# Attention, MoE and routed MoE on one core: the first MoE's cosine as one shifted sine, and the high halves of odd score tiles on ScalarE

## The chip, the cores and the metric

The kernel runs on one core of one Trainium2 chip, as one program. The metric is the time of an execution in microseconds (us), measured on the device. The engines are named as the profile names them: PE is TensorE's matmul, PEld its weight load, DVE is VectorE, ACT is ScalarE, POOL is GpSimd, SP is SyncE, which here only issues DMAs.

## The reference, cut to what matters

```python
# u, v: 8 x 3072 x 256; z: 8 x 3072 x 64
scores = np.matmul(z, z.transpose(0, 2, 1)) / S
out = np.matmul(np.maximum(scores, 0.0) ** 2, v)
x = (u * out).reshape(B * S, D)                  # 24576 tokens x 256
h = x @ w_in                                     # first MoE: 256 -> 2048
x = (h * np.cos(h)) @ w_out                      # 2048 -> 256
# second MoE: every token goes to one of 8 experts (256 -> 1024 -> 256),
# chosen by cosine similarity, with relu, and is scaled by its gate
out[mask] = gate_w[mask, None] * (np.maximum(x[mask] @ w1[e], 0.0) @ w2[e])
```

## The kernel before

**Arithmetic.** All large products are done in fp16 with each factor split in a high half and a low half (hi = round(x), lo = x - hi), and three matmuls for each product: hi*hi, hi*lo, lo*hi. So each product's left factor costs two more passes on the other engines: one that makes the high half, one that subtracts it.

**Tiling.** Tokens are taken in 48 chunks of 512, n = 0 to 47, six to each of the eight batches; c = n mod 6 is the chunk's place in its batch. A chunk's attention needs 24 score tiles of 128 x 512, j = 0 to 23. Scores are symmetric, so chunk c computes only the tiles j = 4c to 23 and reads the others back, transposed, from a copy that an earlier chunk wrote to DRAM. Of the computed tiles the first four lie on the diagonal and are narrower (512, 384, 256, 128 columns).

- A computed tile goes through `att_S` (PE, PSUM tile `sc`), `att_relu` (ACT, L547), `att_a32` (the square, ACT, L554), `att_ahi` (the high half, L569 or L571), `att_alo` (the low half, DVE, L577), and `att_V` (PE, `acc`, L641 to L643).
- A chunk's first MoE runs two chunks later, in 16 slices f of 128 hidden units: `ffn_H` (six matmuls, L709 to L711, into PSUM tile `h`, which has two buffers), `ffn_k` (ACT, L718: h in turns, rounded to an integer), `ffn_f` (DVE, L724: the fraction of a turn), `ffn_sin` (ACT, L731), `ffn_sq` (ACT, L735), `ffn_g` (DVE, L739: (2 sin^2 - 1) * h, which frees `h`), `ffn_ghi` (ACT, L746), `ffn_glo` (DVE, L752), `ffn_O` (twelve matmuls, L767 to L775).
- Then comes the chunk's readout: `ro_evac`, `ro_scale`, `ro_hi`, `ro_lo` build the row that is stored, `ro_T` (SP) transposes it by DMA, `ro_tail` (DVE, L839 and L840) writes the row's tail and must wait until these transposes (`xrT`) have read it, and `ro_logits` and `ro_rank` route the tokens.
- Once per batch, at the end of the batch before, `v_scale` finds the scale of v: a sum on DVE, an all-reduce over partitions on POOL (behind the index scatters of `ro_rank`), and nine small DVE instructions that wait for it (the first is L118).

The second MoE starts after the last chunk, at about 4000 us of the span.

**Order.** The program is written as a list of events with a nominal time each (`tl.at(t, function, n, f)`), sorted by that time, and given to a tile framework. After the first stretch SP's order is the list's; the other engines' instructions are placed by the framework's scheduler, which starts from the list. On the chip each engine runs its instructions strictly in the order in which they stand, so an instruction that waits holds up all that stand behind it.

Of the kernel before, what the change touches and what calls it, by code (L numbers as in the profile page):

```python
# [8 lines left out]
FP32 = mybir.dt.float32  # L9
FP16 = mybir.dt.float16  # L10
I32 = mybir.dt.int32
ACTF = mybir.ActivationFunctionType
ALU = mybir.AluOpType
AX = mybir.AxisListType
PI = 3.141592653589793
# [26 lines left out]
def kernel(  # L42
# [15 lines left out]
    nc = tc.nc  # L58
# [19 lines left out]
    const = ctx.enter_context(tc.tile_pool(name="const", bufs=1))  # L78
# [70 lines left out]
    en_r = const.tile([128, KD, 2 * E], FP16, name="en_r")  # L149
    ienx = const.tile([128, 1], FP32, name="ienx")  # L150
    zrow = const.tile([1, RW // 2], FP32, name="zrow")

    tl = Timeline()

# [40 lines left out]
    def setup_consts():  # L195
        nc.gpsimd.memset(ones16, 1.0)
        ii = small.tile([128, 128], FP32, name="ii", tag="ii")
        nc.gpsimd.iota(
            ii, pattern=[[1, 128]], base=0, channel_multiplier=-1, allow_small_or_imprecise_dtypes=True
        )  # L200

        nc.vector.tensor_scalar(out=lt16, in0=ii, scalar1=0.0, scalar2=None, op0=ALU.is_gt)
        nc.gpsimd.iota(tok_i, pattern=[[CH, NC], [128, TT]], base=0, channel_multiplier=1)
        e_f = small.tile([128, TT, E], FP32, name="e_f", tag="e_f")
        nc.gpsimd.iota(
            e_f, pattern=[[0, TT], [1, E]], base=0, channel_multiplier=0, allow_small_or_imprecise_dtypes=True
        )
        nc.vector.tensor_scalar(
            out=wfirst, in0=e_f, scalar1=-1.0, scalar2=float(E), op0=ALU.mult, op1=ALU.add
        )  # L210
        nc.vector.tensor_scalar(
            out=ecap, in0=e_f[:, 0, :], scalar1=float(CAP), scalar2=None, op0=ALU.mult
        )
        nc.vector.tensor_copy(out=base, in_=ecap)
        nc.vector.memset(zrow, 0.0)
        nc.sync.dma_start(out=xs_d[NT:NT + 1, :], in_=zrow)
        rows = E * CAP + CH
        fill = st_p.tile([128, 512], I32, name="fill", tag="st")
        nc.gpsimd.memset(fill, NT)
        blk = 128 * 512  # L220
        r0 = 0
        while r0 < rows:
            n = min(blk, rows - r0)
            c = n // 128
            nc.sync.dma_start(
                out=idl_d[r0:r0 + n, :].rearrange("(p c) o -> p (c o)", p=128), in_=fill[:, 0:c]
            )
            r0 += n
# [61 lines left out]
    wsc = {}  # L290
# [241 lines left out]
    def att_cols(n, j):  # L532

        return slice((j % 4) * 128 if j // 4 == n % NCB else 0, CH)
# [22 lines left out]
    def att_ahi(n, j):  # L557

        hl = at_p.tile([128, 2 * CH], FP16, name="ahl", tag="ahl", bufs=8)
        a = a_t[n, j]  # L560
        if j // 4 == n % NCB:
            hl = hl.rearrange("p (w c) -> p w c", w=2)
            hi, lo = (hl[:, w, att_cols(n, j)] for w in range(2))
        else:
            a = a.rearrange("p (t c) -> p t c", c=128)
            hl = hl.rearrange("p (t w c) -> p t w c", w=2, c=128)
            hi, lo = (hl[:, :, w] for w in range(2))
        if n < 2 and j % 2:
            nc.scalar.activation(out=hi, in_=a, func=ACTF.Copy)  # L569
        else:  # L570
            nc.vector.tensor_copy(out=hi, in_=a)  # L571
        a_t[n, j] = (a, hi, lo, hl)
# [44 lines left out]
    def att_order(c):  # L617

        load, off = list(range(4 * c)), list(range(4 * c + 4, NJ))

        at = 4 if c else 0
        comp, off = off[:at], off[at:]
        for j in range(4 * c, 4 * c + 4):
            comp += [j, *off[:2]]
            off = off[2:]
        comp += off
        pos = [((i + 0.5) / len(x), j) for x in (load, comp) for i, j in enumerate(x)]
        return [j for _, j in sorted(pos)]
# [19 lines left out]
    u_t, x_t, xsc = {}, {}, {}  # L648
# [49 lines left out]
    h_t, f_t, g_t, o_t = {}, {}, {}, {}  # L698
# [15 lines left out]
        h_t[n, f] = ps  # L714

    def ffn_k(n, f):
        kt = ff_p.tile([128, CH], I32, name="kt", tag="kt", bufs=5)
        nc.scalar.activation(out=kt, in_=h_t[n, f], func=ACTF.Copy, scale=xsc[n][0])  # L718
        f_t[n, f] = kt

    def ffn_f(n, f):
# [4 lines left out]
        )  # L726
        f_t[n, f] = t

    def ffn_sin(n, f):
        t = f_t[n, f]  # L730
        nc.scalar.activation(out=t, in_=t, func=ACTF.Sin, scale=PI)  # L731

    def ffn_sq(n, f):
        t = f_t[n, f]
        nc.scalar.activation(out=t, in_=t, func=ACTF.Square, scale=2.0 ** 0.5)  # L735

    def ffn_g(n, f):
        g = f_t.pop((n, f))
        nc.vector.scalar_tensor_tensor(  # L739
            out=g, in0=g, scalar=1.0, in1=h_t.pop((n, f)), op0=ALU.subtract, op1=ALU.mult  # L740
        )
        g_t[n, f] = [g]

    def ffn_ghi(n, f):
# [38 lines left out]
    def ro_evac(n):  # L783
        x2 = ro_p.tile([128, TT, D], FP32, name="x2", tag="x2")
        o = o_t.pop(n)
        k2 = small.tile([128, 1], FP32, name="k2", tag="k2")
        nc.vector.tensor_scalar(
            out=k2, in0=xsc[n][1], scalar1=wsc[1][1], scalar2=-1.0, op0=ALU.mult, op1=ALU.mult
        )
        for t in range(0, TT, 2):  # L790
            nc.scalar.activation(  # L791
                out=x2[:, t:t + 2], in_=o[TT + t // 2], func=ACTF.Copy, scale=k2
            )
        x2_t[n] = x2
# [151 lines left out]
    def tB(n):  # L946
        return starts[n]

    tl.at(30000, setup_consts)
    for b in range(B):  # L950
        n0 = b * NCB
        if b == 0:
            tl.at2(3700, 3700, z_nat, z_stat, 0)
            for c in range(NCB):
                t = 8600 + 1400 * c if c < 2 else 4000 + 7000 * c
# [10 lines left out]
        else:  # L966
# [7 lines left out]
            for c in range(NCB):  # L974

                t = last + (min((c - NCB + 2) * ZC, 0.1) + (c == NCB - 1) * 0.9) * P
# [23 lines left out]
    for n in range(NC):  # L1000
        t0 = tB(n)
        st = (tB(n + 1) - t0) / NJ
        tl.at(t0 + 0.3 * NJ * st, u_load, n)
        order = att_order(n % NCB)
        for i, j in enumerate(order):
            t = t0 + i * st
            if j // 4 < n % NCB:
                tl.at(t + LV - LM, att_load, n, j)
            else:

                ts = max(t0, t - DV * st) if j // 4 == n % NCB and j % 4 else t
                tl.at(ts, att_S, n, j)
                tl.at(ts + 300, att_relu, n, j)
                tl.at(ts + 1500, att_a32, n, j)
                tl.at(ts + 2000, att_ahi, n, j)
                tl.at(ts + 2400, att_alo, n, j)
                tl.at(max(ts + 6000, t + LV - 5500), att_mirror, n, j)


            if i in (0, NJ - 2):  # L1020
                continue
            js = order[i - 1:i + 1] if i in (1, NJ - 1) else [j]
            tl.at(t + LV + (0, 1000, 700, 0)[min(i, 3)], att_V, n, js, i == 1, i == NJ - 1)
        e = tB(n + 1) - st + LV + 1400
        tl.at(e, x_mul, n)
        tl.at(e + 5000, x_scale, n)
        for k in range(KD):
            tl.at(e + 5500 + 1500 * k, x_hi, n, k)
            tl.at(e + 6500 + 1500 * k, x_lo, n, k)

        tail = n + 2 - NC
        fb = tB(n + 2) + 14000 if tail < 0 else tB(NC) + 12000 + tail * PF
        FP = (tB(n + 3) - tB(n + 2) if tail < 0 else PF) / NF
        LO = (3.2 if tail >= 0 else 3.00) * FP
        for f in range(NF):
            t = fb + f * FP
            tl.at(t, ffn_H, n, f)
            tl.at(t + 1400, ffn_k, n, f)
            tl.at(t + 1800, ffn_f, n, f)
            tl.at(t + 3200, ffn_sin, n, f)  # L1040
            tl.at(t + 3900, ffn_sq, n, f)
            tl.at(t + 4700, ffn_g, n, f)
            tl.at(t + 6600, ffn_ghi, n, f)
            tl.at(t + 8300, ffn_glo, n, f)
            tl.at(t + LO, ffn_O, n, f)
        r = fb + (NF - 1) * FP + LO + 1500
        tl.at(r, ro_evac, n)
        tl.at(r + 2300, ro_scale, n)
        for t in range(TT):
            tl.at(r + 3000 + 2000 * t, ro_hi, n, t)  # L1050
            tl.at(r + 4200 + 2000 * t, ro_lo, n, t)

        late = RT if tail < 0 else 4000.0
        for t in range(TT):
            tl.at(r + 4300 + 2000 * t + late, ro_T, n, t)
        tl.at(r + 11500 + late, ro_tail, n)
        tl.at(r + 17000 + late, ro_logits, n)
        tl.at(r + 27000 + late, ro_rank, n)
        T_RANK[n] = r + 27000 + late
        T_END = r  # L1060
# [303 lines left out]
    for s, (tb, i, n) in enumerate(slots):  # L1364
# [13 lines left out]
        for u in range(nu):  # L1378
            t = t0 + u * fq
# [55 lines left out]
```

## Time and profile before

| | us |
|---|---|
| median of three runs | 5095.66 (5089.55 to 5098.19) |
| the profiled execution | 5086.35 |
| its span, first to last instruction | 5084.6 |
| PE busy | 4885.2 (96% of the span) |
| DVE busy | 3641.9 (72%) |
| ACT busy | 3302.5 (65%) |
| POOL busy | 1509.3 (30%) |

The profile is one execution; its own time is 1.75 us more than its span and 9.3 us under the median of the runs. Busy time says how long an engine worked, waits say which engine it stood still for. An engine's waits matter only if the engine itself is one that the end waits for.

### The profile page before, as it was taken

The numbers are of one execution on the slowest core, as the hardware profiler recorded it, in microseconds if no ns is written. First come the engines' busy times: TensorE is split into PE (matmuls) and PEld (weight loads), VectorE is DVE, ScalarE is ACT, GpSimd is POOL, SyncE is SP. The second block draws the span as 40 slices with busy tenths as digits, with TensorE's granted clock in tenths as the row PEclk, the third lists the DMA queues.
The fourth block names the chain that finished last, engine by engine and source line by source line (L and its number), as shares of the span: only waits on it lengthen the run. The fifth ranks groups of instructions, "written<-read, shape, count | busy, mean of one in ns | idle before, by whom it ended". The sixth has DMA issues, their size and how long they took to land.

```text
span 5084.6 us, 87365 instructions
## 1 busy us (share of the span) xinstructions
PE 4885.2 (96%) x31032; PEld 2935.5 (58%) x31032; DVE 3641.9 (72%) x9258; ACT 3302.5 (65%) x6269; POOL 1509.3 (30%) x2105
## 2 busy tenths in 40 slices
PE   6999999999999999999999999999999799999999
PEld 2555555555555555555555555555556467777776
DVE  6967776777678768776877787777767655656565
ACT  6777777777778778777877787777767422222222
POOL 3232222232233223223322322332121333333332
PEclk9999999999999999999999999999999899999999
DMA  7676468456755675647555844774472667777874
GB/s 225 172 144 119 110 138 135 115 122 132 132 122 130 121 137 121 131 100 151 130 114 111 161 125 95 142 137 111 99 124 54 174 180 212 212 213 219 226 224 129
DMA packets 963689, 731.26 MB, mean 144 GB/s; under 512 B 855696, under 2 KB 858769, under 8 KB 954418
## 3 DMA queue, kind: packets, MB, share of 16 engines
q1 hardware_dynamic: 835490, 351.44, 36.0%
q0 software_dynamic: 127760, 374.24, 26.8%
q8 instruction: 243, 3.98, 0.4%
q14 instruction: 196, 1.61, 0.1%
HBM read 315.17 MB, written 215.19 MB: 104 GB/s over the span
## 4 chain that ended last, share of the span: by engine, by line
PE 63%; ACT 12%; DVE 12%; issue 6%; DMA 5%; POOL 1%; SPq 1%; POOLq 0%; another core or an unknown queue 0%; DVEq 0%; ACTq 0%
PE acc L642 6%; PE acc L643 6%; PE acc L641 6%; PE o L771 4%; PE o L775 4%; PE h L709 4%; PE o L767 4%; PE h L710 4%; PE h L711 4%; PE h L1297 3%; PE o L1334 3%; PE o L1327 3%; PE o L1331 3%; PE h L1289 3%; PE h L1293 3%
## 5 line engine op out<-in xcount | busy, mean ns | idle before, releaser
L767 PE MATMUL o<-wo,gh 128*128 128x256 f16 x3072 | 841.0, 274 | 5.3 <-ACT x L791 4.1
L775 PE MATMUL o<-wo,gl 128*128 128x256 f16 x3072 | 840.6, 274 | 1.7 <-DVE gl L752 1.2
L771 PE MATMUL o<-wo,gh 128*128 128x256 f16 x3072 | 841.4, 274 | 0.0
L746 ACT ACTIVATE gh<-kt 128x512 f16<-128x512 f32 x768 | 482.4, 628 | 458.8 <-DVE kt L739 445.0
L739 DVE SCALAR_TENSOR_TENSOR kt<-kt,h 128x512 f32<-128x512 f32 x768 | 525.9, 685 | 344.1 <-ACT kt L735 332.7
L752 DVE TENSOR_TENSOR gl<-kt,gh 128x512 f16<-128x512 f32 x768 | 528.5, 688 | 223.9 <-ACT gh L746 206.9
L731 ACT ACTIVATE kt<-kt 128x512 f32<-128x512 f32 x768 | 480.4, 626 | 313.0 <-DVE kt L724 303.1
L580 POOL DMA_DIRECT2D at_d<-ahl x480 | 268.5, 559 | 1286.7 <-DVE ahl L577 1044.7
L709 PE MATMUL h<-xh,wi 128*128 128x512 f16 x1536 | 587.6, 383 | 37.8 <-DVE kt L739 36.7
L724 DVE SCALAR_TENSOR_TENSOR kt<-h,c,kt 128x512 f32<-128x512 f32 x768 | 572.9, 746 | 63.3 <-ACT kt L718 59.1
L1306 ACT ACTIVATE hh<-h 128x512 f16<-128x512 f32 x398 | 234.9, 594 | 567.7 <-PE h L1297 470.7
L710 PE MATMUL h<-xl,wi 128*128 128x512 f16 x1536 | 587.5, 382 | 0.0
L711 PE MATMUL h<-xh,wi 128*128 128x512 f16 x1536 | 586.8, 382 | 0.0
L718 ACT ACTIVATE kt<-h,c 128x512 int32<-128x512 f32 x768 | 517.5, 674 | 105.6 <-PE h L711 86.3
L642 PE MATMUL acc<-ahl,vh 128*128 128x512 f16 x1344 | 512.3, 381 | 38.9 <-DVE ahl L577 38.8
L641 PE MATMUL acc<-ahl,vh 128*128 128x512 f16 x1344 | 511.2, 381 | 14.2 <-ACT vh L363 5.7
L1308 DVE SCALAR_TENSOR_TENSOR hl<-h,hh 128x512 f16<-128x512 f32 x398 | 271.7, 687 | 336.8 <-ACT hh L1306 307.4
L643 PE MATMUL acc<-ahl,vl 128*128 128x512 f16 x1344 | 511.7, 381 | 0.0
L735 ACT ACTIVATE kt<-kt 128x512 f32<-128x512 f32 x768 | 481.1, 626 | 14.4
L1334 PE MATMUL o<-w,hl 128*128 128x256 f16 x1592 | 435.4, 274 | 18.0 <-DVE hl L1308 14.2
L1331 PE MATMUL o<-w,hh 128*128 128x256 f16 x1592 | 435.2, 273 | 4.4 <-issue 4.4
L1327 PE MATMUL o<-w,hh 128*128 128x256 f16 x1592 | 435.1, 273 | 3.9 <-issue 3.8
(326 smaller groups left out, 10510.5 us busy)
## 6 DMA issues: line engine op xcount, KB each, us to landing
w<-we_d SPq DMA_DIRECT2D x69, 2048.0 KB
at_d<-ahl POOLq DMA_DIRECT2D x480, 256.0 KB
vst<-in_v POOLq DMA_DIRECT2D x168, 256.0 KB
est<-in_w POOLq DMA_DIRECT2D x128, 256.0 KB
xs_d<-row POOLq DMA_DIRECT2D x48, 544.0 KB
ut<-in_uT POOLq DMA_DIRECT2D x42, 512.0 KB
zst<-in_zT POOLq DMA_DIRECT2D x84, 128.0 KB
ad_d<-ahl POOLq DMA_DIRECT2D x96, 96.0 KB
```

The source lines that it names most:

```text
L641: nc.tensor.matmul(out=acc[k], lhsT=h, rhs=ah, start=beg, stop=False)
L642: nc.tensor.matmul(out=acc[k], lhsT=h, rhs=al, start=False, stop=False)
L643: nc.tensor.matmul(out=acc[k], lhsT=lo, rhs=ah, start=False, stop=end)
L709: nc.tensor.matmul(out=ps, lhsT=wi_hi[:, k, fs], rhs=xh[:, k], start=(k == 0), stop=False)
L710: nc.tensor.matmul(out=ps, lhsT=wi_hi[:, k, fs], rhs=xl[:, k], start=False, stop=False)
L711: nc.tensor.matmul(out=ps, lhsT=wi_lo[:, k, fs], rhs=xh[:, k], start=False, stop=(k == KD - 1))
L767: nc.tensor.matmul(out=o[t], lhsT=gh[:, ts], rhs=wo_hi[:, f], start=(f == 0 and t % 2 == 0), stop=False, skip_group_check=True,)
L771: nc.tensor.matmul(out=o[t], lhsT=gh[:, ts], rhs=wo_lo[:, f], start=False, stop=False, skip_group_check=True,)
L775: pe_last[0] = nc.tensor.matmul(out=o[t], lhsT=gl[:, ts], rhs=wo_hi[:, f], start=False, stop=(f == NF - 1), skip_group_check=True,).ins
L1327: nc.tensor.matmul(out=o[t], lhsT=hh[:, ts], rhs=wh, start=(f == 0 and t % 2 == 0), stop=False, skip_group_check=True,)
L1331: nc.tensor.matmul(out=o[t], lhsT=hh[:, ts], rhs=wl, start=False, stop=False, skip_group_check=True)
L1334: nc.tensor.matmul(out=o[t], lhsT=hl[:, ts], rhs=wh, start=False, stop=(f == NF2 - 1), skip_group_check=True,)
```

## The change

The cosine was made as 1 - 2 sin^2: h is turned into a fraction of a turn in -0.5 to 0.5, ACT takes sin(pi f), squares it with a factor sqrt(2), and DVE computes (that - 1) * h, whose sign the readout's scale `k2` turns back. Now `ffn_k` adds a quarter turn before it rounds, so that the fraction lies in -0.75 to 0.25, ACT takes sin(2 pi f + pi/2) once, and DVE multiplies by h. The quarter and pi/2 are bias operands that stand in SBUF, one number for each partition. `ffn_sq` is gone, and the nominal times of the steps after the sine are 700 ns earlier. Besides, `att_ahi` of odd tiles, which was on ACT only in the first two chunks, is on ACT in all chunks.

```diff
+    quarter = const.tile([128, 1], FP32, name="quarter")
+    half_pi = const.tile([128, 1], FP32, name="half_pi")
...
+        nc.vector.memset(quarter, 0.25)
+        nc.vector.memset(half_pi, PI / 2.0)
...
-        if n < 2 and j % 2:
+        if j % 2:
             nc.scalar.activation(out=hi, in_=a, func=ACTF.Copy)
         else:
             nc.vector.tensor_copy(out=hi, in_=a)
...
-        nc.scalar.activation(out=kt, in_=h_t[n, f], func=ACTF.Copy, scale=xsc[n][0])
+        nc.scalar.activation(
+            out=kt, in_=h_t[n, f], func=ACTF.Identity, scale=xsc[n][0], bias=quarter
+        )
...
-        nc.scalar.activation(out=t, in_=t, func=ACTF.Sin, scale=PI)
-        nc.scalar.activation(out=t, in_=t, func=ACTF.Square, scale=2.0 ** 0.5)
+        nc.scalar.activation(out=t, in_=t, func=ACTF.Sin, scale=2.0 * PI, bias=half_pi)
...
-        nc.vector.scalar_tensor_tensor(
-            out=g, in0=g, scalar=1.0, in1=h_t.pop((n, f)), op0=ALU.subtract, op1=ALU.mult
-        )
+        nc.vector.tensor_tensor(out=g, in0=g, in1=h_t.pop((n, f)), op=ALU.mult)
...
-            out=k2, in0=xsc[n][1], scalar1=wsc[1][1], scalar2=-1.0, op0=ALU.mult, op1=ALU.mult
+            out=k2, in0=xsc[n][1], scalar1=wsc[1][1], scalar2=None, op0=ALU.mult
...
-            tl.at(t + 4700, ffn_g, n, f)
+            tl.at(t + 4000, ffn_g, n, f)
```

The order of PE's matmuls stays nearly the same, and SP's stays the same. DVE's and ACT's orders move at many places. Three of them follow; line numbers in the changed program are two to eight higher.

DVE, at the readout of chunk 7 (c = 1; the same at the other seven chunks with c = 1). Before, with `ffn_g` (L739), a score tile's high half (L571), the row's tail (L839, L840), the same tile's low half (L577), `ffn_glo` (L752) and `ffn_f` (L724):

```order
L739 SCALAR_TENSOR_TENSOR kt<-kt,h 128x512
L571 CAST ahl<-r 128x4x128
L839 COPY row<-amv 128x4x4
L840 COPY row<-ssq 128x4x4
L577 TENSOR_TENSOR ahl<-r,ahl 128x4x128
L752 TENSOR_TENSOR gl<-kt,gh 128x512
L724 SCALAR_TENSOR_TENSOR kt<-h,c_8057,kt 128x512
```

The same place in the changed program (`ffn_g` is L743, `ffn_glo` L754, the low half L581, `ffn_f` L731, the tail L841 and L842):

```order
L743 TENSOR_TENSOR kt<-kt,h 128x512
L754 TENSOR_TENSOR gl<-kt,gh 128x512
L581 TENSOR_TENSOR ahl<-r,ahl 128x4x128
L731 SCALAR_TENSOR_TENSOR kt<-h,c_7950,kt 128x512
L407 TENSOR_REDUCE ewm<-ewst 128x2
L841 COPY row<-amv 128x4x4
L842 COPY row<-ssq 128x4x4
L743 TENSOR_TENSOR kt<-kt,h 128x512
```

The tile is odd, so its high half is no longer here, and its low half, `ffn_glo` and `ffn_f` stand ahead of the tail, not behind it.

DVE, at the readout of chunk 20 (c = 2; the same at chunks 2, 8, 14, 32 and 38, not at 26). Before:

```order
L724 SCALAR_TENSOR_TENSOR kt<-h,c_20570,kt 128x512
L752 TENSOR_TENSOR gl<-kt,gh 128x512
L364 SCALAR_TENSOR_TENSOR vl_21822<-vst,vss,vh_21821 128x512
L839 COPY row<-amv 128x4x4
L840 COPY row<-ssq 128x4x4
L739 SCALAR_TENSOR_TENSOR kt<-kt,h 128x512
```

The changed program (L368 is the low half of a piece of v, as L364 was):

```order
L754 TENSOR_TENSOR gl<-kt,gh 128x512
L841 COPY row<-amv 128x4x4
L368 SCALAR_TENSOR_TENSOR vl_21488<-vst,vss,vh_21487 128x512
L731 SCALAR_TENSOR_TENSOR kt<-h,c_20255,kt 128x512
L842 COPY row<-ssq 128x4x4
L743 TENSOR_TENSOR kt<-kt,h 128x512
```

Here it is the other way round: `ffn_f` of the slice (L731) and the split of v, which stood ahead of the tail, now stand behind its first instruction; the slice's `ffn_g` is the last row in both.

ACT, at the start of batch 4 (chunk 24). Before, with `ffn_k` (L718), two splits of z (L363), `ffn_sin`, `ffn_sq`, `ffn_ghi` (L746), and the first tiles' relu (L547), square (L554):

```order
L363 ACTIVATE r_5_22308<-zst,zps 64x512
L731 ACTIVATE kt<-kt 128x512
L735 ACTIVATE kt<-kt 128x512
L746 ACTIVATE gh<-kt 128x512
L718 ACTIVATE kt<-h,c_20570 128x512
L547 ACTIVATE r<-sc 128x512
L547 ACTIVATE r<-sc 128x384
L554 ACTIVATE r<-r 128x512
L554 ACTIVATE r<-r 128x384
L731 ACTIVATE kt<-kt 128x512
L547 ACTIVATE r<-sc 128x512
```

The changed program (`ffn_cos` is L739, `ffn_k` L723, `ffn_ghi` L748, relu L551, square L558, the high half L573):

```order
L367 ACTIVATE r_5_21963<-zst,zps 64x512
L739 ACTIVATE kt<-kt,half_pi 128x512
L748 ACTIVATE gh<-kt 128x512
L723 ACTIVATE kt<-h,quarter,c_20255 128x512
L551 ACTIVATE r<-sc 128x512
L551 ACTIVATE r<-sc 128x384
L558 ACTIVATE r<-r 128x512
L558 ACTIVATE r<-r 128x384
L739 ACTIVATE kt<-kt,half_pi 128x512
L573 ACTIVATE ahl<-r 128x384
L551 ACTIVATE r<-sc 128x512
```

One instruction fewer stands in front of the first relu; in front of the third the copy of the odd tile has come in.

## Rows read from the trace of the kernel before

**Rows 1.** The page: busy us, share of span, instructions of each engine.

```profile
PE 4885.2 (96%) x31032; PEld 2935.5 (58%) x31032; DVE 3641.9 (72%) x9258; ACT 3302.5 (65%) x6269; POOL 1509.3 (30%) x2105
```

**Rows 2.** Windows: stretch, its length, busy us (count) by engine, clock, DMA, GB/s.

```profile
0.00:200.00 200.00, 145.81 (x660) 66.26 (x661) 144.45 (x313) 139.42 (x262) 66.16 (x113) 0.97 0.78 218
200.00:3900.00 3700.00, 3609.60 (x21732) 2068.81 (x21730) 2788.66 (x6168) 2805.45 (x5305) 1036.70 (x1576) 0.99 0.61 124
```

**Rows 3.** Windows of 100 us each.

```profile
300.00:400.00 100.00, 89.85 (x527) 50.15 (x525) 68.28 (x164) 69.37 (x138) 27.01 (x41) 0.98 0.77 132
...
1600.00:1700.00 100.00, 100.00 (x605) 57.60 (x604) 78.72 (x169) 76.45 (x141) 24.79 (x39) 1.00 0.56 121
...
3300.00:3400.00 100.00, 92.19 (x549) 53.11 (x548) 71.92 (x156) 69.74 (x127) 32.24 (x47) 0.97 0.91 150
```

**Rows 4.** Waits of PE, 200 to 3900: us in total, times, longest.

```profile
PE h L709 <- DVE kt L739: 35.7, 43, 3.9
PE acc L642 <- DVE ahl L577: 28.1, 23, 2.9
PE sc L541 <- ACT r L547: 18.6, 7, 3.2
```

**Rows 5.** Waits of PE at readouts of chunks 1 and 43 (330:352, 3754:3762).

```profile
PE acc L642 <- DVE ahl L577: 3.0, 2, 2.5
...
PE acc L642 <- DVE ahl L577: 1.3, 1, 1.3
```

**Rows 6.** ACT by line and shape, 200 to 3900: busy us, mean ns, idle before.

```profile
L718 ACT ACTIVATE kt<-h,c 128x512 int32<-128x512 f32 x732 | 493.5, 674 | 83.3 <-PE h L711 64.0 <-PE pr L908 8.5 <-issue 6.3
L746 ACT ACTIVATE gh<-kt 128x512 f16<-128x512 f32 x732 | 460.0, 628 | 454.2 <-DVE kt L739 440.9 <-issue 9.1 <-DVE ahl L577 3.0
L735 ACT ACTIVATE kt<-kt 128x512 f32<-128x512 f32 x732 | 458.6, 627 | 14.1
L731 ACT ACTIVATE kt<-kt 128x512 f32<-128x512 f32 x732 | 457.9, 626 | 307.4 <-DVE kt L724 297.9 <-DVE gl L752 3.3 <-issue 2.5
L689 ACT ACTIVATE xh<-x,xss 128x512 f16<-128x512 f32 x92 | 62.9, 712 | 0.4 <-DVE xss L105 0.4
```

**Rows 7.** ACT's high halves of odd tiles, 0 to 200.

```profile
L569 ACT ACTIVATE ahl<-r 128x512 f16<-128x512 f32 x18 | 11.2, 621 | 0.1
```

**Rows 8.** DVE by line and shape, 200 to 3900.

```profile
L752 DVE TENSOR_TENSOR gl<-kt,gh 128x512 f16<-128x512 f32 x731 | 503.2, 688 | 221.1 <-ACT gh L746 204.5 <-issue 11.1 <-PE o L775 3.5
L739 DVE SCALAR_TENSOR_TENSOR kt<-kt,h 128x512 f32<-128x512 f32 x732 | 501.3, 685 | 339.7 <-ACT kt L735 328.6 <-ACT kt L731 5.4 <-issue 0.5
L571 DVE CAST ahl<-r 128x512 f16<-128x512 f32 x480 | 208.4, 434 | 96.1 <-ACT r L554 93.1 <-issue 1.4 <-ACT kt L735 0.2
```

**Rows 9.** Timeline, readout of chunk 7: start us, us, instruction [idle before].

```profile
831.15 0.17 DVE L839 COPY row<-amv 128x16 f32<-128x16 f32 x1 [4.33 <-DMA xrT<-row]
...
832.05 0.38 PE L642 MATMUL acc<-ahl,vh 128*128 128x512 f16 x1 [2.92 <-DVE ahl L577]
```

**Rows 10.** Timeline, readout of chunk 20.

```profile
1890.50 0.17 DVE L839 COPY row<-amv 128x16 f32<-128x16 f32 x1 [2.27 <-DMA xrT<-row]
...
1890.66 0.68 DVE L739 SCALAR_TENSOR_TENSOR kt<-kt,h 128x512 f32<-128x512 f32 x1
...
1891.40 0.38 PE L709 MATMUL h<-xh,wi 128*128 128x512 f16 x1 [0.42 <-DVE kt L739]
```

**Rows 11.** Timeline, behind `v_scale` of batch 4.

```profile
1844.11 0.74 DVE L724 SCALAR_TENSOR_TENSOR kt<-h,c,kt 128x512 f32<-128x512 f32 x1
...
1844.89 0.63 ACT L731 ACTIVATE kt<-kt 128x512 f32<-128x512 f32 x1 [5.25 <-DVE kt L724]
1845.55 0.63 ACT L735 ACTIVATE kt<-kt 128x512 f32<-128x512 f32 x1
...
1846.21 0.69 DVE L739 SCALAR_TENSOR_TENSOR kt<-kt,h 128x512 f32<-128x512 f32 x1 [1.36 <-ACT kt L735]
...
1846.95 0.38 PE L709 MATMUL h<-xh,wi 128*128 128x512 f16 x1 [3.11 <-DVE kt L739]
```

More of the change, by code (lines that the diff above doesn't have):

```diff
@@ L727, in ffn_f, with ffn_cos @@
         f_t[n, f] = t
-    def ffn_sin(n, f):
+    def ffn_cos(n, f):
         t = f_t[n, f]
-        nc.scalar.activation(out=t, in_=t, func=ACTF.Sin, scale=PI)
-    def ffn_sq(n, f):
-        t = f_t[n, f]
-        nc.scalar.activation(out=t, in_=t, func=ACTF.Square, scale=2.0 ** 0.5)
+        nc.scalar.activation(out=t, in_=t, func=ACTF.Sin, scale=2.0 * PI, bias=half_pi)
     def ffn_g(n, f):
         g = f_t.pop((n, f))
-        nc.vector.scalar_tensor_tensor(
-            out=g, in0=g, scalar=1.0, in1=h_t.pop((n, f)), op0=ALU.subtract, op1=ALU.mult
-        )
+        nc.vector.tensor_tensor(out=g, in0=g, in1=h_t.pop((n, f)), op=ALU.mult)
         g_t[n, f] = [g]
@@ L1039 @@
             tl.at(t + 1800, ffn_f, n, f)
-            tl.at(t + 3200, ffn_sin, n, f)
-            tl.at(t + 3900, ffn_sq, n, f)
-            tl.at(t + 4700, ffn_g, n, f)
-            tl.at(t + 6600, ffn_ghi, n, f)
-            tl.at(t + 8300, ffn_glo, n, f)
+            tl.at(t + 3200, ffn_cos, n, f)
+            tl.at(t + 4000, ffn_g, n, f)
+            tl.at(t + 5900, ffn_ghi, n, f)
+            tl.at(t + 7600, ffn_glo, n, f)
             tl.at(t + LO, ffn_O, n, f)
```

## The prediction, made before the changed kernel had run

> **What bounds the kernel now.** I read the page's busy line first: PE is busy 96% of the span, no other engine over 72% [rows 1]. The windows by stage say where PE's rest lies: 54 us in the first 200 us, and 90 us in the 3700 us in which attention and the first MoE run side by side [rows 2]. There PE is simply full for long stretches (100.00 of 100 us, [rows 3]). So the change, which lightens ACT and DVE, can only give back what PE waits for. DVE and ACT are each busy about 76% of that stage (2789 and 2805 us, [rows 2]); neither is the bound by its sum. They hurt where one of them stands still in its queue with something behind it that PE needs.
>
> The waits of PE name these places [rows 4]: 35.7 us in 43 waits for `ffn_g` (it frees PSUM tile `h` for the next-but-one slice), 28.1 us in 23 waits for a tile's low half, 18.6 us in 7 waits for the relu that frees `sc`. That is 82 of the 90 us. The timelines tell their causes. At the readout of chunk 7 DVE stood 4.33 us at the row's tail until the transposes had read the row; a tile's low half stood behind it, and PE waited 2.92 us for it [rows 9]. After `v_scale` DVE had been held up by POOL's reduce; the next slice's fraction, sine, square and product then ran one after the other, and PE waited 3.11 us [rows 11]. On top, in ten of the 37 windows of 100 us the granted clock is not full (spells at 1.2 instead of 2.4 GHz; the first of the ten at 0.98, the last at 0.97, [rows 3]); their shortfalls add up to 24 us.
>
> **The change part by part.** All sums are against the profiled execution, 5086.35 us: its span of 5084.6 and 1.75 us around it. The median of the runs is 9.3 us higher; I carry the gain over to it unchanged.
>
> *Price of the operations.* The square goes: 732 times 627 ns, 459 us of ACT in the stage [rows 6]. The sine and `ffn_k` get a bias operand from SBUF. No row shows an ACTIVATE with two such operands. The nearest: a copy with a scale from SBUF takes 712 ns, without one 628 [rows 6], so 84 ns for one operand. Ends for each of the two: 0 and twice that, 168 ns; below nothing is excluded, since elements, types and passes stay. I take 84 each: 732 x 2 x 84 = 123 us. The high halves: 314 tiles move; a full one costs DVE 434 ns [rows 8] and ACT 621 ns [rows 7], so at most 136 us less on DVE and at most 195 us more on ACT, as the diagonal tiles are narrower. ACT then has 2805 - 459 + 123 + 195 = 2664 us at most, DVE 2653. The product with h is a plain two-input operation now; the nearest row is 688 ns against 685 [rows 8], so nothing. Two memsets and `k2` in one operation instead of two: nothing, PE runs beside them. The order of the changed program has three table loads on ACT as before, so the shift from Copy to Identity adds none.
>
> At this point the Trainium skill speaks against the change. The trace has the fp32 to fp16 high half at 434 ns on DVE and 621 on ACT [rows 7, 8]. The page "VectorE: DVE Perf Modes", section "Mode 2×_2P — use both read ports for one tensor", says why the first is cheap: a copy with one source in SBUF moves two elements a cycle even in fp32. By it the move gives away about 59 us of engine time, and the sum would be better without it. By the trace that engine time lies beside a full PE, and what counts is which instruction stands in which queue.
>
> *Low halves ahead of the tail: -16 us.* At the eight readouts with c = 1 the low half that PE waited for now stands ahead of the tail, as the order shows. Those waits are 3.0 us at chunk 1 and 1.3 at chunk 43 [rows 5], eight in all, together 18.2 us. What is late next is the product and the sine of the slice after; its fraction stands ahead of the tail too, so the product can follow the tail at once. I leave 2 us.
>
> *Low halves still behind the tail: +2 us.* At the seven readouts with c = 4 the low half stays behind the tail, and in five of them the tile's high half has moved behind it as well: five times 434 ns.
>
> *The slice's chain without the square: -12 us.* From the square's start to the product's is 0.66 us [rows 11]. With 84 ns more on the sine, 0.57 us goes. Twelve of the 43 waits for `ffn_g` are longer than that (28.0 of 35.7 us): 12 x 0.57 = 6.8 us. The other 31 hold 7.7 us; I take 5 of it as gone.
>
> *The fraction behind the tail: +9 us.* This is the part that costs. At six readouts with c = 2 the tail's wait now comes ahead of the fraction. At chunk 20 the product followed the tail by 0.16 us, and PE still waited 0.42 for it [rows 10]. Now a split of v (an operation of the fraction's kind and size, so 0.74 us too), the fraction (0.74, [rows 11]) and the sine (0.71) come between: 2.2 us. At chunk 20 all of it shows. At the other five PE did not wait, so it has something in hand there; I take 0.9 us, and 1.3 us shows at each (all of it would be 2.2, nothing would be 0): 2.2 + 5 x 1.3 = 8.7 us. If DVE reaches the tail sooner by what it no longer does ahead of it, nothing changes, since the transposes set the time.
>
> *Waits for the relu: -2 us.* Seven, at the batches' starts; one square less, two bias operands more stand ahead of the relu. PE's wait shrinks by about 0.3 us each, since the product behind two splits on DVE then becomes the late one.
>
> *Clock: -4 us.* Of the 24 us I give back a sixth, where a wait that went before a drop gets shorter.
>
> The sum: -16 + 2 - 12 + 9 - 2 - 4 = -23 us. The start (the first two chunks had their odd halves on ACT already) and the second MoE do not change; the last slices, on a busy ACT, gain a microsecond or so, which then waits for the row's transposes. Forecast: 5063 us for the profiled execution, 5073 for the median. Its own range, with the bias operands at both ends (0.17 us on the chain either way, 12 to 30 places, so 2 to 5 us) and the tail's +9 between 3 and 14: 5058 to 5085.
>
> **The rivals.**
>
> *The gain is larger.* In the 30 to 50 us after a readout with c = 1 the slices run as one ring (k, fraction, sine, square, product, high half, next k), and the waits for `ffn_g` come in rows of three and more. If the ring sets the pace there, 0.57 us less for each slice also lets it catch up before `v_scale`, and most of what is left goes: 18 + 25 of the 35.7 + 4 of the relu's + 14 of the clock's = 61 us, less the 6 that the tail may still cost: 55. The median would be 5041. For it: ACT's 307 us of waits for the fraction and DVE's 329 for the square [rows 6, 8] show the ring closed. Against it: the big waits each start from a DVE that stood still, not from the ring.
>
> *The waits move.* The low half gets ahead of the tail, but the slice's own steps are late there as well, so 18 us turn into waits for `ffn_g`; with the +9 of the fraction and 168 ns for each bias operand the change gives 4 us: 5092. For it: after the wait of [rows 9] the next waits were for `ffn_g`, if short. Against: the fraction stands ahead there now.
>
> *Slower: odd tiles wait for ACT.* Until now an odd tile's high and low half followed each other on DVE. Now the low half waits for a copy that stands in ACT's queue behind a slice's steps, among them a high half that itself waits for DVE (441 us in all, [rows 6]). Each tile's low half comes later by 0.19 us of the copy and one step of 0.63. Where PE waits for it, that is 0.82 us; 314 tiles have it. It breaks even with the forecast's 23 us at 28 more tiles, one in eleven. At one in five it takes 63 x 0.82 = 52 us, and 52 - 23 = +29: 5125. Against it: PE now waits at 23 of 672 tiles, and `att_V` comes several tiles after its scores.
>
> That the change doesn't do what it says I exclude, as the square is gone from the order.
>
> **How the numbers follow.** Forecast 0.48, larger gain 0.22, waits move 0.18, slower 0.12. What a measurement of this kernel can tell from no change is about 0.2%, 10 us. Faster: 0.48, 0.22 and a little of the third, less the forecast's own upper end at 5085: 0.71. Same: 0.18. Slower: 0.11. The range leaves out the slow rival and the far end of the larger gain: 5036 to 5098.
>
> **What would show it.** Right: the waits for the low half fall from 28 us to 10 to 14, at c = 1 to nearly none; the waits for `ffn_g` fall to about 33 us with new ones of 1 to 2 us right behind the tail at c = 2; the sine takes about 712 ns and `ffn_k` about 760; PE is full where it was full. Wrong: waits for the low half over 25 us (then the odd tiles wait for ACT or the order helps nothing), waits for `ffn_g` under 15 us (then the ring set the pace), or a change in the stretches in which PE was at 100 of 100 us, which no term here provides for.

## The result, and the profile after

The changed kernel takes 5039.05 us (median; 5037.17 to 5043.64), the kernel before, run beside it, 5096.41 us (5089.55 to 5098.19): a ratio of 0.9891, 95% interval 0.9874 to 0.9908, so about 57 us less where 23 were forecast. The profiled execution takes 5037.17 us, its span is 5035.4 us, 49.2 less than the span before.

The busy line of the page answers to [rows 1], the window to [rows 2].

```profile
PE 4872.0 (97%) x31032; PEld 2934.1 (58%) x31032; DVE 3553.7 (71%) x8946; ACT 3169.4 (63%) x5815; POOL 1509.1 (30%) x2105
```

```profile
200.00:3900.00 3700.00, 3646.67 (x22118) 2102.41 (x22117) 2750.72 (x5984) 2729.15 (x4970) 1043.02 (x1582) 1.00 0.61 125
```

PE has the same instructions and, in the same 3700 us, gets through 386 more of them. Waits of PE in that window, against [rows 4] (us in total, times, longest):

```profile
PE h L713 <- DVE kt L743: 35.2, 20, 5.5
PE acc L646 <- DVE ahl L581: 5.0, 10, 1.9
PE acc L645 <- DVE ahl L575: 3.4, 4, 1.2
PE acc L645 <- DMA ahl<-ad_d: 3.0, 3, 1.6
PE acc L645 <- DMA alm<-at_d: 2.9, 1, 2.9
PE sc L545 <- ACT r L551: 1.3, 3, 0.6
```

The waits for `ffn_g` are as long as before, in half as many places. Those for a tile's halves fell from 28.1 to 8.4 us, those for the relu from 18.6 to 1.3. From the first slice of the first MoE to the first slice of its last chunk it is 3776.8 us before and 3718.7 after, 58 less: waits for the low halves 19 less, for the relu 19, for `ro_evac` (ACT's copy of `o`, which the next chunk's `ffn_O` waits for) 4; waits for DMAs 4 more; the clock's shortfall (length times what the granted clock lacked) 23.9 before, 11.9 after. The rest, about 7, is spread thinly. The second MoE did not change. The start, up to the first slice, took 8 us longer in the profile (150.6 and 158.8); more on that below.

The operations by line and shape (busy us, mean ns, idle before), against [rows 6 to 8]:

```profile
L723 ACT ACTIVATE kt<-h,quarter,c 128x512 int32<-128x512 f32 x752 | 578.2, 769 | 183.4 <-PE h L715 163.2 <-PE pr L910 8.6 <-issue 7.4
L739 ACT ACTIVATE kt<-kt,half_pi 128x512 f32<-128x512 f32 x750 | 538.0, 718 | 309.6 <-DVE kt L731 301.3 <-DVE t0cum L1102 0.9 <-issue 0.8
L573 ACT ACTIVATE ahl<-r 128x512 f16<-128x512 f32 x218 | 135.3, 621 | 2.1
```

```profile
L743 DVE TENSOR_TENSOR kt<-kt,h 128x512 f32<-128x512 f32 x750 | 512.5, 683 | 235.9 <-ACT kt L739 225.6 <-issue 4.4
```

A bias operand costs 95 ns on `ffn_k` (769 against 674) and 92 on the sine (718 against 626), where 84 each were taken. The product is as long as before, a full odd high half takes 621 ns on ACT, as priced.

**One place before and after.** At the start of batch 4, PE computes the first scores, ACT's relu frees `sc`. The timeline before (start us, length, instruction, in brackets the idle time ahead):

```profile
1926.17 0.38 PE L541 MATMUL sc<-r 128*128 128x512 f16 x1
...
1928.75 0.63 ACT L746 ACTIVATE gh<-kt 128x512 f16<-128x512 f32 x1 [0.75 <-DVE kt L739]
1929.28 0.67 ACT L718 ACTIVATE kt<-h,c 128x512 int32<-128x512 f32 x1
...
1929.85 0.97 ACT L547 ACTIVATE r<-sc 128x512 f32<-128x512 f32 x2
1930.49 0.38 PE L541 MATMUL sc<-r,r 128*128 128x512 f16 x1 [2.96 <-ACT r L547]
```

and after:

```profile
1903.08 0.63 ACT L748 ACTIVATE gh<-kt 128x512 f16<-128x512 f32 x1 [0.87 <-DVE kt L743]
...
1903.43 0.38 PE L545 MATMUL sc<-r 128*128 128x512 f16 x1
1903.63 0.78 ACT L723 ACTIVATE kt<-h,quarter,c 128x512 int32<-128x512 f32 x1
...
1904.31 0.97 ACT L551 ACTIVATE r<-sc 128x512 f32<-128x512 f32 x2
1904.95 0.38 PE L545 MATMUL sc<-r,r 128*128 128x512 f16 x1
```

The relu stands in the same place of ACT's queue, behind a slice's high half and the next slice's `ffn_k`. Before, these two came 2.6 and 3.1 us after PE's scores, since the slices were late behind PE; the relu ran 3.7 us after the scores. After, the slices had caught up: the high half began 0.35 us ahead of the scores, the relu ran 0.9 us after them, and PE hardly waited (under 0.1 us). At the starts of batches 1 to 7 the relu ran 2.8 to 3.9 us after the first scores before, and 0.9 to 1.4 us after.

### The profile page after: what moved, and what is told of

Same layout as the page of the kernel before. It is cut to its first block, busy times and chain, and to the rows that moved or that the text cites. A ratio compares the mean times of both kernels' runs of the same rounds, so it can differ in the third digit from the quotient of the medians.

```text
span 5035.4 us, 86979 instructions
## 1 busy us (share of the span) xinstructions
PE 4872.0 (97%) x31032; PEld 2934.1 (58%) x31032; DVE 3553.7 (71%) x8946; ACT 3169.4 (63%) x5815; POOL 1509.1 (30%) x2105
## 4 chain that ended last, share of the span: by engine, by line
PE 66%; ACT 10%; DVE 9%; issue 7%; DMA 5%; POOL 2%; SPq 1%; POOLq 0%; DVEq 0%; ACTq 0%
PE acc L646 6%; PE acc L647 6%; PE acc L645 6%; PE h L713 4%; PE h L715 4%; PE h L714 4%; PE o L769 4%; PE o L777 4%; PE o L773 4%; PE h L1298 3%; PE o L1335 3%; PE o L1328 3%; PE o L1332 3%; PE h L1290 3%; PE h L1294 3%
## 5 line engine op out<-in xcount | busy, mean ns | idle before, releaser
L739 ACT ACTIVATE kt<-kt,half_pi 128x512 f32<-128x512 f32 x768 | 550.9, 718 | 313.6 <-DVE kt L731 305.1
L748 ACT ACTIVATE gh<-kt 128x512 f16<-128x512 f32 x768 | 480.2, 626 | 422.0 <-DVE kt L743 409.6
L723 ACT ACTIVATE kt<-h,quarter,c 128x512 int32<-128x512 f32 x768 | 590.4, 769 | 205.8 <-PE h L715 165.4
L754 DVE TENSOR_TENSOR gl<-kt,gh 128x512 f16<-128x512 f32 x768 | 528.9, 689 | 258.7 <-ACT gh L748 246.1
L743 DVE TENSOR_TENSOR kt<-kt,h 128x512 f32<-128x512 f32 x768 | 524.7, 683 | 237.1 <-ACT kt L739 226.6
L731 DVE SCALAR_TENSOR_TENSOR kt<-h,c,kt 128x512 f32<-128x512 f32 x768 | 574.0, 747 | 161.6 <-ACT kt L723 145.8
L713 PE MATMUL h<-xh,wi 128*128 128x512 f16 x1536 | 585.6, 381 | 36.1 <-DVE kt L743 35.2
L581 DVE TENSOR_TENSOR ahl<-r,ahl 128x512 f16<-128x512 f32 (+3 forms) x672 | 421.3, 631 | 33.8 <-ACT ahl L573 23.6
```

What stands on the lines that cost most here:

```text
L713: nc.tensor.matmul(out=ps, lhsT=wi_hi[:, k, fs], rhs=xh[:, k], start=(k == 0), stop=False)
L723: nc.scalar.activation(out=kt, in_=h_t[n, f], func=ACTF.Identity, scale=xsc[n][0], bias=quarter)
```

## The experiments

Theory: in ACT's order a slice's high half stands ahead of the next slice's `ffn_k`, so the slices run as one closed ring (`ffn_k`, `ffn_f`, sine, square, `ffn_g`, `ffn_ghi`, next `ffn_k`). From the start of `ffn_k` to the end of `ffn_g` it took at least 3.50 us before and 3.02 after (the smallest of 736 slices). A whole turn of the ring, counted where nothing else held the next `ffn_k` (the high half started within 0.15 us of the end of `ffn_g`, the next `ffn_k` right behind it, the next `h` was ready), took 4.62 us before and 4.11 after in the median; PE took 5.04 and 4.96 us for a slice on average. An estimate from these four numbers: late slices caught up with PE by about 0.4 us a slice before and 0.85 after. There were 214 such turns among 690 before and 110 after. A shorter ring lets slices that a stop of DVE made late catch up with PE before the next place where something else stands behind them. The rivals: A, the lighter DVE; B, the order that came from the earlier nominal times; C, the lighter ACT. Each kernel was timed beside the kernel before on the same chip; the chips differ (medians of the kernel before 5082 to 5113 us), so ratios are compared.

**The two parts apart.**

```diff
-        if j % 2:
+        if n < 2 and j % 2:
```

> The cosine part alone: one sine with a quarter turn more, odd high halves back on VectorE. Theory (the slice's ring got shorter than PE's slice, so slices that are late catch up before the next batch or readout): PE's waits for the relu at the batches' starts fall from 18.6 us to under 4, those for ScalarE's readout copy vanish, the clock's shortfall is 10 to 14 us; the waits for a tile's low half stay at 20 us or more. Time about 5062 (30 to 40 us under the kernel before). Rival A (the relief of VectorE by the moved high halves did it): waits for the relu stay at 15 us or more, time 5080 to 5095. Rival B (the earlier nominal times alone moved the low halves): waits for low halves fall to 10 here too, time about 5040.

Measured: 5045.22 us, ratio 0.9928 (0.9912 to 0.9944). Waits of PE, 200 to 3900:

```profile
PE h L713 <- DVE kt L743: 36.5, 24, 3.2
PE acc L646 <- DVE ahl L581: 13.3, 14, 3.1
...
PE acc L645 <- DVE ahl L575: 2.4, 3, 1.0
PE sc L545 <- ACT r L551: 1.6, 3, 0.7
```

The relu's waits go with the cosine alone, and the time is 37 us under the kernel before on this chip. The clock's shortfall, 17.1, is above the 10 to 14 expected. The waits for halves fall further than the theory had it, to 15.7 us, between it and rival B: at the readout of chunk 7 the low half now runs at 826.19, ahead of the tail at 832.24. So that part of the gain came with the cosine as well, by the place in DVE's order.

The other part, in the kernel before:

```diff
-        if n < 2 and j % 2:
+        if j % 2:
```

> The move of the odd high halves alone; sine and square as in the kernel before. Theory: the ring of a slice keeps its square (and ScalarE gets 195 us more work), so waits for the relu stay at 15 us or more, the clock's shortfall at 20 or more; the low halves' waits fall by at most half. Time 5085 to 5110. Rival A (relief of VectorE): waits for low halves and for the relu both fall, time 5045 to 5065.

Measured: 5083.12 us, ratio 0.9997 (0.9986 to 1.0007).

```profile
PE h L709 <- DVE kt L739: 36.4, 34, 2.8
PE acc L642 <- DVE ahl L577: 30.8, 22, 2.7
PE sc L541 <- ACT r L547: 15.0, 7, 3.0
```

The same readout in its timeline:

```profile
834.56 0.18 DVE L839 COPY row<-amv 128x16 f32<-128x16 f32 x1 [4.34 <-DMA xrT<-row]
834.79 0.69 DVE L577 TENSOR_TENSOR ahl<-r,ahl 128x512 f16<-128x512 f32 x1
835.54 0.59 PE L642 MATMUL acc<-ahl,vh 128*128 128x512 f16 x1 [2.67 <-DVE ahl L577]
```

The low half stays behind the tail, and no wait shrinks much. Rival A falls as the cause by itself: DVE had some 100 us less to do in that window, for nothing. But the two parts together give 0.9891, more than their product 0.9925. With the short ring the move of the high halves is worth something: the next run has both parts, was timed on the same chip as the cosine alone, and is 18 us faster (0.9893 against 0.9928, the intervals apart). Whether that comes from the lighter DVE or from the order is not shown.

**The nominal times.**

```diff
-            tl.at(t + 4000, ffn_g, n, f)
-            tl.at(t + 5900, ffn_ghi, n, f)
-            tl.at(t + 7600, ffn_glo, n, f)
+            tl.at(t + 4700, ffn_g, n, f)
+            tl.at(t + 6600, ffn_ghi, n, f)
+            tl.at(t + 8300, ffn_glo, n, f)
```

> The changed kernel with the old nominal times of the three steps behind the cosine (700 ns later each), so with an order nearer to that of before. Theory (ring length): waits for the relu stay under 4 us, the low halves' waits may come back (10 to 28 us): time 5039 to 5058. Rival B (order by nominal times): half of the gain or more is lost, time 5068 or more.

Measured: 5026.94 us on a chip where the kernel before takes 5082.2, ratio 0.9893 (0.9877 to 0.9909): the changed kernel's own. Waits for the relu are 0.4 us, for halves 12.1. The waits for `ffn_g` are 23.5 us and those for DMAs 17.5, against 35.2 and 5.9 in the changed kernel, at the same ratio. The earlier times did nothing to the time that can be measured, and rival B falls.

**The ring as long as it was, and ACT as busy without it.** First a pass in the square's place:

```diff
+    def ffn_pass(n, f):
+        t = f_t[n, f]
+        nc.scalar.activation(out=t, in_=t, func=ACTF.Copy)
...
             tl.at(t + 3200, ffn_cos, n, f)
+            tl.at(t + 3900, ffn_pass, n, f)
```

> The changed kernel with one more ScalarE pass over the cosine (a copy onto itself) in the square's place, due at the same point; nothing else differs, and its result doesn't either. Theory (ring length): the ring is as long as before or 0.2 us longer, so waits for the relu come back to 15 us or more, the clock's shortfall to 20 or more: 5080 to 5125. Rivals A and B (VectorE's relief, or the order): PE's waits stay as they are, time 5035 to 5050.

Then a pass at the same nominal time that no step of the slice reads:

```diff
+    def ffn_side(n, f):
+        jk = ro_p.tile([128, D], FP16, name="jk", tag="jk")
+        nc.scalar.activation(
+            out=jk.bitcast(mybir.dt.float8e4), in_=wi_hi[:, 0, 0:CH], func=ACTF.Copy, saturate=False
+        )
...
             tl.at(t + 3200, ffn_cos, n, f)
+            tl.at(t + 3900, ffn_side, n, f)
```

> The changed kernel with one more ScalarE pass for each slice of the first MoE, of the length of the square that went (512 columns), but on data that nothing waits for: as much work for ScalarE as with the pass over the cosine, and not in the slice's chain. Theory (the length of the chain, not ScalarE's load): most of the gain stays, 5035 to 5065, waits for the relu under 8 us. Rival C (ScalarE's load in the stage): as slow as with the pass in the chain, 1.008 of the kernel before, 5110 or more, waits for the relu 15 us or more.

Measured: with the pass in the chain 5123.9 us, ratio 1.0084 (1.0069 to 1.0099), chain 3.68 us; with the pass beside it 5043.33 us, ratio 0.9907 (0.989 to 0.9924), chain 3.02. The passes (ACT by line, 200 to 3900) and the waits of PE, in the chain:

```profile
L743 ACT ACTIVATE kt<-kt 128x512 f32<-128x512 f32 x718 | 447.7, 624 | 11.0
```

```profile
PE h L713 <- DVE kt L747: 44.8, 35, 5.3
PE acc L646 <- DVE ahl L581: 39.0, 28, 3.2
PE sc L545 <- ACT r L551: 19.9, 7, 3.9
PE o L773 <- ACT x L797: 11.5, 13, 1.6
```

and beside the chain:

```profile
L743 ACT ACTIVATE jk<-wi 128x512 fp8e4<-128x512 f16 x737 | 438.6, 627 | 0.0
```

```profile
PE h L713 <- DVE kt L749: 34.9, 35, 3.0
PE acc L646 <- DVE ahl L581: 11.6, 19, 2.0
PE sc L545 <- ACT r L551: 8.0, 7, 1.9
```

ACT is as busy in one as in the other (3024 and 3052 of the 3700 us, more than in the kernel before). In the chain the pass brings back every wait that the change had taken away, and more, as the bias operands stay; beside the chain it costs next to nothing (0.9907 against the changed kernel's 0.9897 on that chip). Rival C falls. The turns that nothing but the ring held go the same way: 219 of 690 with the pass in the chain, 85 with it beside. The relu's 8.0 us are at the theory's bound: at batch 4 it runs 2.1 us after PE's scores (3.7 before, 0.9 after), so a fuller ACT has a small part in it. With the pass in the chain the low half stands behind the tail again, at seven of the eight readouts with c = 1: the framework's scheduler made another order for the longer chain, so the chip's part and the order's part are not separated here.

**The ring opened.** On ACT the next slice's `ffn_k` is put ahead of this slice's high half, in the changed kernel and then in the kernel before (there from 6600 and 8300 to the same nominal times). The first added line is in `ffn_k`, the second in `ffn_ghi`:

```diff
+        k_ins[n, f] = nc.scalar.activation(
...
+        with tc.issue_after(k_ins[n, min(f + 1, NF - 1)]):
...
-            tl.at(t + 5900, ffn_ghi, n, f)
-            tl.at(t + 7600, ffn_glo, n, f)
+            tl.at(t + 7200, ffn_ghi, n, f)
+            tl.at(t + 8900, ffn_glo, n, f)
```

> The changed kernel with the next slice's first step (h in turns) put ahead of this slice's high half on ScalarE, so that it no longer waits for this slice's product. Theory (ring length): the slices can follow each other faster still, waits for ffn_g fall from 35 us to 15 to 28, time 5015 to 5035. Rival (the ring is already short enough, and what is left are single stops of VectorE): waits for ffn_g stay at 30 or more, 5035 to 5050.

Measured: 5007.65 us, ratio 0.9838 (0.9822 to 0.9853), better than expected; the changed kernel, once more beside it, 0.9897 (below). Its timeline and its waits of PE:

```profile
1868.79 0.78 ACT L724 ACTIVATE kt<-h,quarter,c 128x512 int32<-128x512 f32 x1 [1.38 <-PE h L716]
1869.47 0.62 ACT L750 ACTIVATE gh<-kt 128x512 f16<-128x512 f32 x1
1869.60 0.75 DVE L732 SCALAR_TENSOR_TENSOR kt<-h,c,kt 128x512 f32<-128x512 f32 x1 [1.28 <-ACT kt L724]
1870.39 0.72 ACT L740 ACTIVATE kt<-kt,half_pi 128x512 f32<-128x512 f32 x1 [0.30 <-DVE kt L732]
```

```profile
PE lg L863 <- DMA xrT<-row: 14.5, 1, 14.5
PE acc L645 <- DMA ahl<-ad_d: 13.0, 4, 6.2
PE acc L645 <- DMA alm<-at_d: 7.2, 5, 3.8
...
PE h L714 <- DVE kt L744: 0.4, 1, 0.4
```

`ffn_k` now waits for PE's `ffn_H`, not for a product, and the high half fills ACT's time beside DVE's fraction. Waits for `ffn_g` went from 35 us to 0.4, though DVE still stood behind POOL's reduce for 9.6 us in all; PE now waits for the transposed score tiles. The first of the rows, 14.5 us at the logits of a readout behind the stage, is not new: it was 11.8 us before, about 50 us behind the first slice of the last chunk in both, and has only come inside the window.

> The kernel before (with its square, its high halves and its sine) and one thing else: the next slice's first step stands ahead of this slice's high half on ScalarE, so that the slices no longer wait for one another there. Theory (the closed ring of a slice is what held PE, not ScalarE's or VectorE's load): waits for ffn_g under 10 us, for the relu under 5, time 0.984 to 0.990 of the kernel before (about 5015 to 5045), so as much as the whole change or more. Rival (the work that the change took away counts by itself): 0.995 or more, about 5065 or more.

Measured: 5028.41 us against 5113.42, ratio 0.9846 (0.9822 to 0.987).

```profile
PE acc L641 <- DMA ahl<-ad_d: 16.3, 4, 7.8
PE h L710 <- DVE kt L742: 15.1, 14, 3.5
```

With the square, with all its work on ACT and DVE, and a chain as long as it was (3.51 us), the kernel before gains as much as the whole change or more; its waits for the relu are 1.9 us from the first slice to the last chunk's (20.5 in the kernel before). The waits for `ffn_g`, 15.1, miss the expected 10. It isn't only the ring that changed: in the scheduler's order for this kernel, too, the low half stands ahead of the tail at all eight readouts with c = 1, and PE waits for no half of a computed tile in the window. So it is in every profile here: the waits for halves are 26 to 41 us in the four that have the low half behind the tail at seven or eight of these readouts (the kernel before, twice; the high halves alone; the pass in the chain), and at most 16 us in the others, which have it ahead at seven or eight. That part of the gain goes with the place in DVE's order.

What the ring leaves PE in hand shows in the time from the end of `ffn_g` to the start of the `ffn_H` that it frees (median over the freed slices 8 to 15 of the first 46 chunks, c of the chunk that the slices belong to, us):

| chunk's place c | before | after | before, opened | after, opened |
|---|---|---|---|---|
| 2 | 0.20 | 0.36 | 2.17 | 3.33 |
| 3 | 1.17 | 2.93 | 3.84 | 4.34 |

After the stops of c = 2 the shorter ring recovers by c = 3, at whose end a new batch's relu stands; the opened ring recovers at once.

**A ring still shorter.**

```diff
-            out=kt, in_=h_t[n, f], func=ACTF.Identity, scale=xsc[n][0], bias=quarter
+            out=kt, in_=h_t[n, f], func=ACTF.Copy, scale=xsc[n][0]
...
-        nc.scalar.activation(out=t, in_=t, func=ACTF.Sin, scale=2.0 * PI, bias=half_pi)
+        nc.scalar.activation(out=t, in_=t, func=ACTF.Sin, scale=PI)
```

> The changed kernel without the two bias operands (the quarter turn is left out of the computation, the sine is taken as in the kernel before), so a slice's chain is 0.19 us shorter still. Theory: the slices catch up a little sooner; PE's waits for ffn_g 28 to 35 us, time 5028 to 5042. If the ring still set the pace for long stretches: 20 us or more less than the changed kernel, 5020 or less.

Measured: 5053.52 us against 5113.42, ratio 0.9891 (0.9872 to 0.991), chain 2.83 us. Another 0.19 us less is worth nothing that can be measured; by this run the closed ring no longer sets the pace for long stretches. But the waits for `ffn_g` rose to 47.3 us in 32 places where they should have fallen, with the clock's shortfall at 17.1; why, these runs don't tell.

**What is left.**

```diff
-            back(last - 0.05 * P, v_scale, b)
+            back(last - 0.15 * P, v_scale, b)
```

> The changed kernel with v_scale due 8 us earlier in its batch, so that GpSimd's reduce stands ahead of the four index scatters instead of behind them. Expected: VectorE's wait for the reduce (27.6 us over the batches) falls under 8 us, PE's waits for ffn_g from 35 us to 12 to 20, the clock's shortfall by some us: 5010 to 5025. Rival: the scatters or another stop of VectorE take its place, waits for ffn_g stay over 28 us, 5035 or more.

Measured: 5023.86 us, ratio 0.9858 (0.9843 to 0.9873). DVE's wait, which had been 27.6 us (16.8 put down to POOL, 10.8 without a releaser), and PE's:

```profile
DVE vsc L118 <- POOL vsr L138: 1.9, 5, 0.4
```

```profile
PE h L713 <- DVE kt L743: 16.7, 14, 4.2
```

About half of the waits for `ffn_g` that stayed after the change came from these stops of DVE behind POOL's scatters (in the changed kernel 22.6 of the 35.2 us came after such a stop and before the next tail); PE's waits for DMAs in the stage rose from 6 to 16 us.

The opened ring, the early `v_scale` and a tail that stands shortly before the logits, together:

```diff
-        tl.at(r + 11500 + late, ro_tail, n)
+        back(r + 16000 + late, ro_tail, n)
```

> The changed kernel with the next slice's first step ahead of the high half, v_scale 8 us earlier, and the row's tail placed shortly before the logits instead of right behind the split, so that VectorE doesn't stand for the transposes. Expected: VectorE's wait at the tail falls from 90 us to under 25, PE's waits for ffn_g and low halves together to under 5 us; PE's waits for transposed score tiles (20 us with the first edit alone) stay. Time 4995 to 5008. Rival: the later tail holds up the logits, PE waits there: over 5010.

Measured: 4999.03 us against 5113.42, ratio 0.9788 (0.9765 to 0.9811), the fastest here.

```profile
PE acc L645 <- DMA ahl<-ad_d: 21.8, 4, 11.1
PE lg L863 <- DMA xrT<-row: 10.4, 1, 10.4
```

```profile
DVE row L843 <- DMA xrT<-row: 18.1, 1, 18.1
```

Of PE's waits in the stage hardly any but the first row's, for transposed score tiles, are left (21.8 of 24.4 us). The second row is again the logits behind the stage, no longer than before, so the rival falls. DVE's wait at the tail went from 90 us to 18.1, one single wait.

**The same kernels once more.**

> The changed kernel once more, for comparison on the same chip with the runs beside it. Time about 0.989 of the kernel before. In its profile, from the first score to the first slice of the first MoE: 156 to 160 us if the 158.8 us seen once belongs to the order, about 150 if it was chance.

> The kernel before once more, for its profile. If the 8 us that the changed kernel lost between the first score and the first slice of the first MoE were chance, this stretch lies between 153 and 164 us here too instead of the 150.6 us seen once; if they belong to the order, it is 151 again.

Measured: the changed kernel 5040.91 us, ratio 0.9897 (0.9882 to 0.9911); the kernel before, one execution, 5104.08 us. Counted from the start of the span, as the 158.8 and 150.6 were, the start up to the first slice takes 163.2 us in the one and 156.2 in the other, and 153.4 to 163.7 in the other kernels. The first profile's 150.6 was the shortest of all. So the same program's start varies by several us; that the changed kernel starts later isn't shown. In the stage the second profile of the kernel before has nearly the same waits as [rows 4]:

```profile
PE h L709 <- DVE kt L739: 35.8, 39, 4.6
PE acc L642 <- DVE ahl L577: 26.1, 21, 2.8
PE sc L541 <- ACT r L547: 18.3, 7, 3.2
```

## Why the prediction was wrong

- **What bounds the kernel** was read rightly: a full PE with 90 us of waits, and a change that can only give some of them back. The median measured, 34 us under the forecast's 5073, is at the lower end of the range of 5036 to 5098.
- **The prices** held: 92 and 95 ns for a bias operand (84 taken). The Trainium skill, "ScalarE: Activation LUTs", section "What ACT_TABLE_LOAD costs", gives about 93 ns for each such operand; the trace agrees. The chain lost 0.48 us, not the 0.57 of the sum, which had left out the operand on `ffn_k`, in the same chain.
- **Low halves, -16 and +2**: measured -19 or -20. At c = 1 the waits went from 18.2 us to 1.0, as forecast; the others went from 9.9 to 7.4, where 2 more were forecast. That they get ahead of the tail belongs to the cosine part, by the two parts apart, which the prediction had not said.
- **The slice's chain, -12, and the fraction behind the tail, +9**: together -3 forecast, -0.5 measured for `ffn_g`. That the sum is nearly right is luck. Put down to the stop of DVE that came last before them, the waits behind `v_scale` went from 24.5 us in 11 places to 22.6 in 7: the first wait behind such a stop was 1.5 to 3.9 us in seven batches before and 3.1 to 5.5 in six after, so the long ones that stayed did not get shorter; of second waits (1.2 to 2.0 us) there were three before and one after. Those behind the tail at c = 2 went from 2.9 to 3.3 us, not up by 9. Those behind the tail at c = 1 went from 7.5 to 9.2: many of 0.2 to 0.3 us went, and new ones came right behind the tail, such as 1.08 us at 825.87. The early `v_scale` shows that about half of what stayed came from DVE's stops at POOL.
- **The failed step** is the chain's: it took 0.57 us off each long wait for `ffn_g`, as if each stood alone, and those waits did not get shorter by that. A closed ring that is nearly as long as PE's slice (4.62 us to 5.04) keeps a delay for tens of us, and hands it on to whatever stands behind it on ACT. So the terms that rested on single waits were too small: the relu -2 (measured -17 to -19), `ro_evac` 0 (-4), the clock -4 (-12). These three make 27 to 29 of the missing 34 us; the clock's share is the least sure, as two executions of the kernel before lie 5 us apart in it. The pass in the chain brought all three back, and the opened ring took them away without the change, each with an order of its own.
- **The rivals.** "The gain is larger" had this mechanism and named 5041 us, but that its number came so near is luck: it had 25 us of `ffn_g`'s waits go (0.5 did) and 4 of the relu's (17 did). So its sign, "under 15 us" for `ffn_g`, was chosen badly. Those waits stayed at 35, most of them right behind a stop of DVE; the ring showed itself at the relu. "Odd tiles wait for ACT" falls by the high halves alone (0.9997) and by the result. "The waits move" falls by the result: 20 us of waits for halves went, and the sum for `ffn_g` did not grow. The dearer copy on ACT, which the prediction held against the move, did not show in the time there (0.9997).
- **What stays open**: how much of the gain is the chip's shorter ring and how much the other order that the scheduler makes of it. The two change together in each kernel here; a kernel with the order of after and a longer chain was not tried. For the low halves, a third of the gain in the stage, the place in DVE's order goes with the waits in every profile; for the relu, whose place in ACT's queue is the same before and after in the rows shown, the shorter ring is what fits, but what other orders in the queues add is not excluded.

## What to carry to other kernels

Where engines with fixed orders hand work round in a circle, compare the circle's length with the period of the engine that bounds: if it is nearly as long, a delay is carried on to the next shared place, and a cut can be worth more than the waits at which it is read. Look first whether an instruction can be moved so that the circle isn't closed at all: one reordering on ACT, with what the scheduler made of it, gave here at least as much as removing a pass of 627 ns from each of 768 slices. An engine's share of busy time says little on this: a pass of 624 ns in the circle cost nearly 2% of the time, and one of 627 ns beside it nothing measurable.

## What the runs showed of the hardware that was not expected

- A copy of 512 columns on ACT takes 627 ns from fp16 to 8-bit floats and 624 ns from fp32 to fp32: the width of the data made no difference between these two.
- The shortfall of PE's clock in the stage goes with PE's waits only roughly: 23.9 and 29.0 us in two executions of the kernel before, 11.9 in both of the changed one, 34.1 with the pass in the chain, but 3.4 with the pass beside it, at 64 us of waits, and 11.9 in the fastest kernel, at 24.
